# Attention on VectorE: one product instruction for two token columns instead of one for each

## The chip, the cores and the metric

The kernel runs on one core of a Trainium2 chip. The metric is the device time of one execution in microseconds (us); shown are single executions, their median, and one further execution that the hardware profiler recorded. The engines are called as the profile calls them: PE (TensorE, matrix multiplication), DVE (VectorE, elementwise work and reductions), ACT (ScalarE), POOL (GpSimd) and SP (SyncE, which issues most loads).

## The reference

One transformer layer with pre-normalization: 2048 tokens of width 576, 32 heads of 18, everything in fp32. Attention is local and dilated: each token looks at itself and 7 tokens behind it, two positions apart. The MLP is gated by a sigmoid and 4608 wide.

```python
idx = pos[:, None] - off[None, :]            # off = arange(8) * 2
mask = idx >= 0
...
logits = jnp.einsum("bhsd,bhswd->bhsw", q, kg) * scale
logits = jnp.where(mask[None, None, :, :], logits, -1e9)
attn = _softmax(logits, axis=-1)
o = jnp.einsum("bhsw,bhswd->bhsd", attn, vg)
...
h = x + _A_ref(_layernorm(x, axis=-1), A_wqkv, A_wo)
h2 = h + _B_ref(_layernorm(h, axis=-1), B_w_gate, B_w_up, B_w_down)
```

Here `_A_ref` is the attention with its projections, `_B_ref` the MLP.

## The kernel before

With a dilation of two, even and odd tokens never meet, so the sequence is handled as two streams of 1024. Each stream is cut into two halves, which gives four blocks of 512 tokens, numbered 0 to 3 (`BLOCKS`). In a block, each of the 128 partitions holds four tokens that follow one another in the stream (the token columns, `j` = 0 to 3), and K and V of 11 tokens (the four and the seven before them). The heads are handled in four groups of 8 heads, 144 columns each.

`attention` does one block and one group on DVE: for each token column it multiplies a window of 8 K rows by `q` (L174, 128x1152 products), for two columns at a time it sums the products over the head's 18 columns (a reduction, L177), then comes the softmax (L185 to L191, its exponential on ACT at L187), for each column the products of 8 V rows with the weights (L200, again 128x1152), and for two columns at a time three additions (L205, L207, L208). There are 4 blocks x 4 groups = 16 such calls, with 64 K products and 64 V products. The function is a generator: at each `yield` it hands over to the code that interleaves it with other work, so the number of yields in a call sets how attention is spread in the order in which the program is written.

PE's matrix products are made of fp32 numbers split into a high and a low part: `split` lets ACT write the high part (L105) and DVE the low part (L106, source minus high part); `split_rest` does the same for the odd 64 columns (L109, L110). So nearly every matmul needs an earlier ACT and DVE instruction.

In time there are four stages. To about 180 us the kernel makes the layer norm and Q, K, V. From there to about 222 us it makes the output projection and second layer norm of block 0 (the generator `front`; `proj_j` adds the projection to the residual at L245). Then the MLP begins (L576 and L583 are the up and gate products, L694 the down products, L702 their eviction by ACT, L598 to L672 the additions between products). While the MLP of the first tokens runs, attention for the last two blocks is made in its shadow (about 400 to 780 us), and then, in the function `under_rest`, their output projections (`proj_scr`; its operands `th`, `tl` are the split attention output, `wow` a projection weight). After the first projection is written, `under_rest` clears a tile on POOL (L906) and ACT's queue issues two DMAs of these zeros to DRAM (L908).

The program is written in Python order with priorities (`high_priority`), and a list scheduler with a simulated clock decides, when the kernel is built, in which order each engine's instructions stand. On the chip, each engine runs its list in that order; an instruction whose inputs or buffers aren't ready holds up everything behind it on its engine. Most weight buffers have one or two copies: `w2` and `w4` (parts of the MLP's weight slice) have one, `w1` two; `b1`, `b2`, `b3` and `bgp` are PSUM banks of PE.

Of the kernel before, what the change touches and what calls it, by code (L numbers as in the profile page):

```python
# [18 lines left out]
ALU = mybir.AluOpType  # L19
AX = mybir.AxisListType  # L20

P = 128
# [3 lines left out]
DH = 18  # L26
W = 8
# [9 lines left out]
HG = NH // NG  # L37
CG = HG * DH
# [23 lines left out]
def kernel(ctx, tc, x, wqkv, wo, wmlp, out):  # L62
    nc = tc.nc
    dve, act, pool, pe, sp = nc.vector, nc.scalar, nc.gpsimd, nc.tensor, nc.sync
# [92 lines left out]
    def window(s, hf):  # L157
        a = s[hf * TB:hf * TB + TB, :].rearrange("(p j) c -> p (j c)", p=P)
        return bass.AP(tensor=a.tensor, offset=a.offset, ap=[[NS * CG, P], [1, (NS + LP) * CG]])

    def attention(at, b, g, o):
        e, hf = BLOCKS[b]
        q = at.tile([P, NS, CG], F32, name="q")
        kw = at.tile([P, NS + LP, CG], F32, tag="kv", bufs=3, name="kw")
        vw = at.tile([P, NS + LP, CG], F32, tag="kv", bufs=3, name="vw")
        sp.dma_start(q.rearrange("p j c -> p (j c)"), qscr[b][g])
        sp.dma_start(kw.rearrange("p j c -> p (j c)"), window(kscr[e][g], hf))
        sp.dma_start(vw.rearrange("p j c -> p (j c)"), window(vscr[e][g], hf))
        lg = at.tile([P, NS, W, HG], F32, bufs=2, name="lg")
        for u in range(2):  # L170
            pr = at.tile([P, 2, W, CG], F32, name="pr")
            for i in range(2):
                j = 2 * u + i
                dve.tensor_tensor(pr[:, i], kw[:, j:j + W],  # L174
                                  q[:, j].unsqueeze(1).broadcast_to([P, W, CG]), ALU.mult)
                yield
            dve.tensor_reduce(lg[:, 2 * u:2 * u + 2].rearrange("p j w h -> p (j w h)"),  # L177
                              pr.rearrange("p j w (h d) -> p (j w h) d", d=DH),
                              AX.X, ALU.add)
            yield  # L180
        if hf == 0:
            dve.tensor_tensor(lg, lg, mask.unsqueeze(3).broadcast_to([P, NS, W, HG]), ALU.add)
        mx = sm.tile([P, NS, HG], F32, name="mx")
        rs = sm.tile([P, NS, HG], F32, name="rs")
        dve.tensor_reduce(mx, lg.rearrange("p j w h -> p j h w"), AX.X, ALU.max)  # L185
        dve.tensor_tensor(lg, lg, mx.unsqueeze(2).broadcast_to([P, NS, W, HG]), ALU.subtract)
        act.activation(lg, lg, AF.Exp, scale=SCALE)  # L187
        yield
        dve.tensor_reduce(rs, lg.rearrange("p j w h -> p j h w"), AX.X, ALU.add)
        dve.reciprocal(rs, rs)  # L190
        dve.tensor_tensor(lg, lg, rs.unsqueeze(2).broadcast_to([P, NS, W, HG]), ALU.mult)  # L191
        yield
        spill = o is None
        if spill:
            o = kw[:, 0:NS]
        for u in range(2):
            pr = at.tile([P, 2, W, CG], F32, name="pr")
            for i in range(2):
                j = 2 * u + i
                dve.tensor_tensor(  # L200
                    pr[:, i].rearrange("p w (h d) -> p w h d", d=DH),
                    vw[:, j:j + W].rearrange("p w (h d) -> p w h d", d=DH),
                    lg[:, j].unsqueeze(3).broadcast_to([P, W, HG, DH]), ALU.mult)
                yield
            dve.tensor_tensor(pr[:, :, 0:4], pr[:, :, 0:4], pr[:, :, 4:8], ALU.add)  # L205
            yield
            dve.tensor_tensor(pr[:, :, 0:2], pr[:, :, 0:2], pr[:, :, 2:4], ALU.add)  # L207
            dve.tensor_tensor(o[:, 2 * u:2 * u + 2], pr[:, :, 0], pr[:, :, 1], ALU.add)  # L208
            yield
        if spill:  # L210
            pool.dma_start(oscr[b][:, :, g * CG:(g + 1) * CG], o)
            if g == NG - 1:
                pool.dma_start(oscr[b][:, :, D:DX], o[:, :, CG - DR:CG])
# [106 lines left out]
    def load_x(b):  # L320
        e, hf = BLOCKS[b]
        t = sah.tile([P, NS, D], F32, bufs=2, name="h")
        for j in range(NS):
            sp.dma_start(t[:, j], xv[e, hf][:, j])
        return t
# [25 lines left out]
    def qkv_w(g):  # L351
        w = qw_tile("qw")
        if g == 0:
            wr = f32(qw_tile("wr"))[:, 0]
        for c in range(5):
            ws = wr[:, c] if g == 0 else sas.tile([P, NQ], F32, tag="wst", bufs=3, name="ws")
            sp.dma_start(ws, wqkv[g][:, c * NQ:(c + 1) * NQ])
            with tc.high_priority(3 * HI if g == 0 else HI):
                split(w[:, 0, c], w[:, 1, c], ws)
        return w  # L360
# [21 lines left out]
    def att_all():  # L382
        nonlocal o
        for b, g in ((0, 0), (0, 1), (0, 2), (0, 3), (1, 0), (1, 1), (1, 2), (1, 3)):
            while (b, g) not in emitted:
                yield
            if o is None:
                o = tok_tile()
            yield from attention(at, b, g, None if b else o[:, :, g * CG:(g + 1) * CG])
            if (b, g) == (0, 3):  # L390
                for j in range(NS):
                    dve.tensor_copy(o[:, j, D:DX], o[:, j, DM:D])
                ready.append(b)
# [28 lines left out]
    w = [qkv_w(0)]  # L422
# [19 lines left out]
    h = load_x(0)  # L442
# [96 lines left out]
    def d_tile():  # L539
        return gd.tile([P, 2, D], F32R, bufs=4, name="d")  # L540
# [239 lines left out]
    def att_scr(at, blocks):  # L780
        for b in blocks:
            for g in range(NG):
                for _ in attention(at, b, g, None):
                    yield ATT
# [171 lines left out]
    with tc.high_priority(2 * HI):  # L956
        wg2 = load_gu(1, pool)
        d = d_tile()
# [126 lines left out]
    for c, (kind, p, f) in enumerate(items):  # L1085
        w, d = wc
# [40 lines left out]
        else:  # L1127
# [22 lines left out]
            d = M[f]  # L1150
# [55 lines left out]
```

## Time and profile before

| | |
|---|---|
| three runs, median (lowest to highest) | 1584.2 us (1582.86 to 1586.56) |
| the profiled execution's own time | 1582.11 us |
| its span, first to last instruction | 1580.3 us |
| mean granted PE clock | 0.998 |
| PE busy | 1548.5 us, 98% of the span |
| DVE busy | 1257.2 us, 80% |
| ACT busy | 879.8 us, 56% |
| POOL busy | 192.4 us, 12% |

The profile records one execution. "Busy" is the time in which an engine worked on an instruction; the span is what passes between the first and the last of them. The granted clock is the share of its full speed that PE was allowed.

### The profile page before, as it was taken

What the parts mean: (1) busy time and instruction counts of PE and PEld (TensorE: products, weight loads), DVE (VectorE), ACT (ScalarE), POOL (GpSimd) and SP (SyncE); (2) the same over time, 40 slices, a digit from 0 to 9 for tenths busy, and PEclk for the clock granted to TensorE, in tenths of its full rate; (3) what the DMA queues carried; (4) which work ended last, traced back from release to release, by engine and by line L of the source; (5) the groups of instructions that cost most, each with busy time, mean ns of one, the idle gap of its engine ahead of it and who ended that gap; (6) DMA issues with size and microseconds to landing.
All of it is one profiled execution on the core that took longest, in us unless ns stands there. A gap on an engine that the chain in (4) does not pass through costs nothing.

```text
span 1580.3 us, 22467 instructions
## 1 busy us (share of the span) xinstructions
PE 1548.5 (98%) x8532; PEld 1377.6 (87%) x8532; DVE 1257.2 (80%) x1979; ACT 879.8 (56%) x1573; POOL 192.4 (12%) x233
## 2 busy tenths in 40 slices
PE   7999989999999999999999999999999999999998
PEld 6899978898788888888888988888888888888888
DVE  7998999657999999999836678777776777776754
ACT  6422245544555565656543345676766777766772
POOL 2000000000010001000011100111111222121121
PEclk9999999999999999999999999999999999999999
DMA  7555576754476666675785225788798899888987
GB/s 268 192 189 193 191 258 192 199 175 160 129 191 163 159 164 163 179 185 141 203 255 191 97 75 141 149 163 178 154 186 171 172 181 188 176 175 179 175 145 193
DMA packets 77405, 278.23 MB, mean 176 GB/s; under 512 B 7952, under 2 KB 13840, under 8 KB 76400
## 3 DMA queue, kind: packets, MB, share of 16 engines
q0 software_dynamic: 29760, 112.96, 39.0%
q1 hardware_dynamic: 39360, 141.93, 26.4%
q10 hardware_dynamic: 8176, 21.89, 3.7%
q8 instruction: 67, 1.10, 0.3%
q14 instruction: 42, 0.34, 0.1%
HBM read 145.88 MB, written 133.23 MB: 177 GB/s over the span
## 4 chain that ended last, share of the span: by engine, by line
PE 87%; DVE 5%; issue 3%; DMA 2%; ACT 2%; POOL 0%; ACTq 0%; SPq 0%; DVEq 0%; POOLq 0%
PE b L576 42%; PE dp L694 14%; PE dp L766 11%; PE acc L152 8%; PE b L583 8%; PE bgp L152 1%; PE b L152 1%; DMA oj<-o 1%; PE acc L154 1%; PE acc L155 1%; DVE pr L174 1%; DVE w L106 1%; DMA ws<-in_wqkv_dram 1%; DVE lg L177 0%; DVE pr L200 0%
## 5 line engine op out<-in xcount | busy, mean ns | idle before, releaser
L576 PE MATMUL b<-tl,w 128*128 128x512 f32 x1716 | 454.3, 393 | 9.1 <-DVE w L106 5.1
L576 PEld LDWEIGHTS b<-tl,w 128*128 128x128 f32 x1716 | 310.7, 188 | 65.3 <-DVE w L106 5.8
L576 PE MATMUL b<-th,w 128*128 128x512 f32 x1368 | 357.2, 392 | 0.8 <-DVE s L672 0.6
L576 PEld LDWEIGHTS b<-th,w 128*128 128x128 f32 x1368 | 251.3, 188 | 48.7 <-DVE s L672 1.1
L772 ACT ACTIVATE ev<-dp 128x576 f32<-128x576 f32 x224 | 145.8, 651 | 114.8 <-PE dp L766 89.6
L583 PE MATMUL b<-th,w 128*128 128x512 f32 x572 | 179.7, 390 | 0.0
L105 ACT ACTIVATE w<-wg 128x640 fp32r<-128x640 f32 (+2 forms) x197 | 117.0, 596 | 93.2 <-PE b L583 60.0
L106 DVE TENSOR_TENSOR w<-wg,w 128x640 fp32r<-128x640 f32 (+2 forms) x197 | 127.4, 649 | 50.2 <-ACT w L105 49.9
L775 POOL DMA_DIRECT2D h<-ev x128 | 109.1, 852 | 452.0 <-ACT ev L772 441.2
L152 PE MATMUL acc<-qw,th 128*128 128x432 f32 x512 | 154.9, 363 | 1.1 <-ACT qw L105 1.1
L583 PEld LDWEIGHTS b<-th,w 128*128 128x128 f32 x572 | 107.1, 188 | 21.5
L694 PE MATMUL dp<-d,h1h 128*128 128x288 f32 x640 | 123.0, 295 | 0.0
L694 PE MATMUL dp<-d,h0h 128*128 128x288 f32 x640 | 122.5, 295 | 0.3 <-DVE tail L704 0.3
L106 DVE TENSOR_TENSOR w<-tw,w 128x512 fp32r<-128x512 f32 x116 | 79.5, 686 | 38.0 <-ACT w L105 37.9
L694 PEld LDWEIGHTS dp<-d,h0h 128*128 128x128 f32 x640 | 101.5, 188 | 6.3 <-DVE tail L704 0.6
L694 PEld LDWEIGHTS dp<-d,h1h 128*128 128x128 f32 x640 | 101.4, 188 | 5.4
L105 ACT ACTIVATE w<-tw 128x512 fp32r<-128x512 f32 x116 | 73.2, 631 | 53.7 <-PE b L576 41.5
L702 ACT ACTIVATE stage<-dp 128x576 f32<-128x576 f32 x112 | 71.2, 648 | 56.4 <-PE dp L694 55.8
L152 PEld LDWEIGHTS acc<-qw,th 128*128 128x128 f32 x512 | 96.7, 189 | 5.8 <-ACT qw L105 1.4
L369 ACT ACTIVATE ev<-acc 128x432 f32<-128x432 f32 x64 | 33.6, 531 | 112.6 <-PE acc L155 110.4
L152 PE MATMUL acc<-qw,tl 128*128 128x432 f32 x256 | 92.2, 360 | 0.4 <-DVE tl L106 0.4
L672 DVE TENSOR_TENSOR s<-s,b 128x512 f32<-128x512 f32 x58 | 39.6, 683 | 62.3 <-PE b L583 62.2
(278 smaller groups left out, 2955.0 us busy)
## 6 DMA issues: line engine op xcount, KB each, us to landing
h<-ev POOLq DMA_DIRECT2D x96, 576.0 KB, 7.2
wg<-in_wmlp_dram SPq DMA_DIRECT2D x49, 928.0 KB, 6.4
h<-stage POOLq DMA_DIRECT2D x28, 1152.0 KB, 11.4
wg<-in_wmlp_dram SPq DMA_DIRECT2D x36, 640.0 KB, 4.9
kw<-kv SPq DMA_DIRECT2D x16, 792.0 KB, 4.2
vw<-kv SPq DMA_DIRECT2D x16, 792.0 KB, 6.1
wd<-in_wmlp_dram SPq DMA_DIRECT2D x18, 576.0 KB, 8.9
kv<-ev ACTq DMA_DIRECT2D x16, 576.0 KB, 5.8
```

Source lines behind the costliest of these rows:

```text
L105: act.activation(hi, src, AF.Copy)
L106: splits.append(dve.tensor_tensor(lo, src, f32(hi), ALU.subtract))
L152: pe.matmul(ps[:, :n], a[:, c, js], m[:, c], start=k == 0, stop=False)
L369: act.activation(ev[:, :, j], ps[:, :NQ].rearrange("p (t c) -> p t c", t=3), AF.Copy)
L576: pe.matmul(ps, wt[:, a, k0 + c], xx[:, m + c], start=first and k == 0, stop=k == 5, skip_group_check=True)
L583: pe.matmul(ps, wt[:, a, k0], xx[:, 4], start=False, stop=a == 1, skip_group_check=True)
L672: added[0] = dve.tensor_tensor(s2, s2, b3, ALU.add)
L694: pe.matmul(ps[:, i, :DH2], a[:, js], d[:, m, i * DH2:(i + 1) * DH2], start=k == 0, stop=k == n)
L702: act.activation(hv, ps, AF.Copy)
L766: pe.matmul(ps[:, i, :DH2], a[x][:, js], m[y], start=k in (0, 1, 3) and q == 0, stop=q == 2, skip_group_check=True)
L772: act.activation(hs[:, k % 2], ps[:, :, :DH2], AF.Copy)
L775: pool.dma_start(hsev[:, u, k0:k + 1], hs[:, :k + 1 - k0], accum_op=ALU.add, max_dma_last_dim=8 * D)
```

## The change

The two products of a pair of token columns become one instruction, for K and for V. Their windows overlap (column j reads rows j to j+7, column j+1 rows j+1 to j+8), so the new helper `taps` writes an access pattern by hand: a first dimension of two columns, one row (144 elements) apart, over the window of 8 rows. The operands `q` and the weights `lg` are broadcast over two columns at once. Each call of `attention` has 4 product instructions of 128x2304 in place of 8 of 128x1152, and 12 yields in place of 16.

```diff
+    def taps(t, j, n):
+        a = t[:, j:j + W]
+        return bass.AP(tensor=a.tensor, offset=a.offset,
+                       ap=[list(a.ap[0]), [CG, 2], [n, W * CG // n], [1, n]])
+
...
             pr = at.tile([P, 2, W, CG], F32, name="pr")
-            for i in range(2):
-                j = 2 * u + i
-                dve.tensor_tensor(pr[:, i], kw[:, j:j + W],
-                                  q[:, j].unsqueeze(1).broadcast_to([P, W, CG]), ALU.mult)
-                yield
+            dve.tensor_tensor(pr, taps(kw, 2 * u, CG),
+                              q[:, 2 * u:2 * u + 2].unsqueeze(2).broadcast_to([P, 2, W, CG]), ALU.mult)
+            yield
...
             pr = at.tile([P, 2, W, CG], F32, name="pr")
-            for i in range(2):
-                j = 2 * u + i
-                dve.tensor_tensor(
-                    pr[:, i].rearrange("p w (h d) -> p w h d", d=DH),
-                    vw[:, j:j + W].rearrange("p w (h d) -> p w h d", d=DH),
-                    lg[:, j].unsqueeze(3).broadcast_to([P, W, HG, DH]), ALU.mult)
-                yield
+            dve.tensor_tensor(
+                pr.rearrange("p j w (h d) -> p j (w h) d", d=DH), taps(vw, 2 * u, DH),
+                lg[:, 2 * u:2 * u + 2].rearrange("p j w h -> p j (w h)").unsqueeze(3)
+                .broadcast_to([P, 2, W * HG, DH]), ALU.mult)
+            yield
```

With fewer yields and fewer instructions the scheduler writes another order. Line numbers of the changed kernel: K product L177, its reduction L180, maximum L188, subtraction L189, V product L201, additions L206, L208, L209; from there on each line is one further down (L245 becomes L246). The numbers behind a name (`pr_1649`) tell one use of a buffer from another and differ between the two programs.

The first place is DVE ahead of the front, around 170 to 188 us, in the last attention group before it. `wow` is the projection weight that is split there, `tl` the low part of the front's transposed attention output. Before, from the max of the softmax on (the three `wow` splits stand ahead of it) and then from the end of the first V product on:

```order
L106 TENSOR_TENSOR wow_1719<-ws_1728,wow_1719 128x288
L185 TENSOR_REDUCE mx_1584<-lg_1524 128x32
L186 TENSOR_TENSOR lg_1524<-lg_1524,mx_1584 128x256
...
L205 TENSOR_TENSOR pr_1608<-pr_1608 128x2x576
L207 TENSOR_TENSOR pr_1608<-pr_1608 128x2x288
L208 TENSOR_TENSOR kw_1519<-pr_1608 128x288
L106 TENSOR_TENSOR tl_1820<-mm_1821,th_1819 128x4x128
L200 TENSOR_TENSOR pr_1649<-vw_1520,lg_1524 128x1152 x2
L110 TENSOR_TENSOR th_1819<-mm_1861,th_1819 64x128
```

And of the change at the same place:

```order
L188 TENSOR_REDUCE mx_1389<-lg_1347 128x32
L189 TENSOR_TENSOR lg_1347<-lg_1347,mx_1389 128x256
L106 TENSOR_TENSOR wow_1749<-ws_1750,wow_1749 128x288
...
L206 TENSOR_TENSOR pr_1413<-pr_1413 128x2x576
L208 TENSOR_TENSOR pr_1413<-pr_1413 128x2x288
L209 TENSOR_TENSOR kw_1342<-pr_1413 128x288
L201 TENSOR_TENSOR pr_1434<-vw_1343,lg_1347 128x2304
L106 TENSOR_TENSOR tl_1841<-mm_1842,th_1840 128x4x128
L110 TENSOR_TENSOR th_1840<-mm_1882,th_1840 64x128
```

The maximum and the subtraction have moved ahead of the three `wow` splits, and the group's second V product from behind the first `tl` split to ahead of it.

The second place is DVE at the start of the MLP, around 229 to 237 us. `s` is the addition that reads PSUM bank `b2` for the last time before PE writes it again; `w1`, `w4`, `w2` are the low parts of the second weight slice. Before:

```order
L598 TENSOR_TENSOR s_2318<-s_2318,b2_2289 128x512
L177 TENSOR_REDUCE lg_2307<-pr_2308 128x128
L174 TENSOR_TENSOR pr_2322<-kw_2302,q_2301 128x1152 x2
L106 TENSOR_TENSOR w1_2273<-wg_2266,w1_2273 128x640
L106 TENSOR_TENSOR w4_2276<-wg_2266,w4_2276 128x384
L106 TENSOR_TENSOR w2_2277<-wg_2266,w2_2277 128x256
L106 TENSOR_TENSOR w1_2353<-wg_2271,w1_2353 128x640
L177 TENSOR_REDUCE lg_2307<-pr_2322 128x128
```

Of the change:

```order
L180 TENSOR_REDUCE lg_1639<-pr_1640 128x128
L599 TENSOR_TENSOR s_2343<-s_2343,b2_2322 128x512
L177 TENSOR_TENSOR pr_1659<-kw_1634,q_1633 128x2304
L106 TENSOR_TENSOR w1_2306<-wg_2299,w1_2306 128x640
L106 TENSOR_TENSOR w4_2309<-wg_2299,w4_2309 128x384
L180 TENSOR_REDUCE lg_1639<-pr_1659 128x128
L106 TENSOR_TENSOR w2_2310<-wg_2299,w2_2310 128x256
L106 TENSOR_TENSOR w1_2376<-wg_2304,w1_2376 128x640
```

One reduction has moved ahead of `s`, the other ahead of the `w2` split.

The third place is around 812 to 830 us, in `under_rest`, where ACT's queue issues the two DMAs of zeros. ACT before:

```order
L105 ACTIVATE w1_7948<-wg_7601 128x640
L105 ACTIVATE w2_7756<-wg_7486 128x256
L109 ACTIVATE th_7378<-bgp_7702 128x128
L702 ACTIVATE stage_7656<-dp_7833 128x576
L908 DMA h7_100<-stage_8151 128x3x576 x2
L105 ACTIVATE w4_7755<-wg_7486 128x384
```

ACT of the change:

```order
L105 ACTIVATE w1_7884<-wg_7537 128x640
L909 DMA h7_100<-stage_8087 128x3x576 x2
L703 ACTIVATE stage_7592<-dp_7769 128x576
L105 ACTIVATE w2_7692<-wg_7422 128x256
L105 ACTIVATE w4_7691<-wg_7422 128x384
```

The DMA issue has moved ahead of the eviction and of the high part of `w2`. And DVE there, which makes the low parts and the projection's additions to the residual (`hj`, L245); before:

```order
L106 TENSOR_TENSOR w2_7756<-wg_7486,w2_7756 128x256
L110 TENSOR_TENSOR th_7378<-bgp_7702,th_7378 64x128
L245 TENSOR_TENSOR hj_7579<-hj_7579,b3_7706 128x288
L125 BN_STATS bs_7914<-hj_7579 128x6
L245 TENSOR_TENSOR hj_7628<-hj_7628,bgp_7736 128x288
L245 TENSOR_TENSOR hj_7671<-hj_7671,b3_7775 128x288
L598 TENSOR_TENSOR s_7799<-s_7799,b2_7768 128x512
L106 TENSOR_TENSOR w4_7755<-wg_7486,w4_7755 128x384
L106 TENSOR_TENSOR d_7762<-wg_7486,d_7762 128x576
L106 TENSOR_TENSOR h1l_7895<-s_7799,h1h_7894 128x512
L245 TENSOR_TENSOR hj_7700<-hj_7700,bgp_7801 128x288
```

Of the change:

```order
L246 TENSOR_TENSOR hj_7515<-hj_7515,b3_7642 128x288
L125 BN_STATS bs_7850<-hj_7515 128x6
L246 TENSOR_TENSOR hj_7564<-hj_7564,bgp_7672 128x288
L106 TENSOR_TENSOR w2_7692<-wg_7422,w2_7692 128x256
L246 TENSOR_TENSOR hj_7607<-hj_7607,b3_7711 128x288
L246 TENSOR_TENSOR hj_7636<-hj_7636,bgp_7737 128x288
L599 TENSOR_TENSOR s_7735<-s_7735,b2_7704 128x512
L106 TENSOR_TENSOR w4_7691<-wg_7422,w4_7691 128x384
```

The `w2` split, which was ahead of all four residual additions, now has the last two behind it; the addition behind the `w4` split has gone from there.

## Rows read from the trace of the kernel before

**Rows 1.** The page: the span, and each engine's busy time, share and instructions.

```profile
span 1580.3 us, 22467 instructions
...
PE 1548.5 (98%) x8532; PEld 1377.6 (87%) x8532; DVE 1257.2 (80%) x1979; ACT 879.8 (56%) x1573; POOL 192.4 (12%) x233
```

**Rows 2.** Window: PE, PEld, DVE, ACT, POOL busy us; clock, DMA, GB/s.

```profile
440.00:760.00 320.00, 320.00 (x1767) 283.18 (x1767) 303.52 (x410) 186.16 (x309) 27.39 (x26) 1.00 0.65 169
```

**Rows 3.** VectorE's groups by form: shapes, count, busy us, mean ns, idle before.

```profile
L200 DVE TENSOR_TENSOR pr<-vw,lg 128x1152 f32<-128x1152 f32 x64 | 84.2, 1354 | 0.5
L174 DVE TENSOR_TENSOR pr<-kw,q 128x1152 f32<-128x1152 f32 x64 | 84.1, 1352 | 0.4
L177 DVE TENSOR_REDUCE lg<-pr 128x128 f32<-128x2304 f32 x32 | 81.5, 2547 | 0.3
```

**Rows 4.** VectorE's timeline at 102 us: start, us, line, tiles, merged count.

```profile
102.14 2.63 DVE L174 TENSOR_TENSOR pr<-kw,q 128x1152 f32<-128x1152 f32 x2
104.80 2.55 DVE L177 TENSOR_REDUCE lg<-pr 128x128 f32<-128x2304 f32 x1
107.39 2.63 DVE L174 TENSOR_TENSOR pr<-kw,q 128x1152 f32<-128x1152 f32 x2
```

**Rows 5.** VectorE's timeline before and in the front; idle before in brackets.

```profile
169.65 1.20 DVE L106 TENSOR_TENSOR wow<-ws,wow 128x288 fp32r<-128x288 f32 x3 [1.76 <-ACT wow L105]
...
172.37 0.68 DVE L189 TENSOR_REDUCE rs<-lg 128x32 f32<-128x256 f32 x1 [0.49 <-ACT lg L187]
...
174.46 0.46 DVE L106 TENSOR_TENSOR wow<-ws,wow 128x288 fp32r<-128x288 f32 x1 [0.57 <-ACT wow L105]
...
181.40 2.62 DVE L200 TENSOR_TENSOR pr<-vw,lg 128x1152 f32<-128x1152 f32 x2
...
232.74 2.63 DVE L174 TENSOR_TENSOR pr<-kw,q 128x1152 f32<-128x1152 f32 x2
235.29 2.36 DVE L106 TENSOR_TENSOR w<-wg,w 128x640 fp32r<-128x640 f32 x4
```

**Rows 6.** TensorE's timeline in the front and at the MLP's start.

```profile
184.49 0.37 PE L152 MATMUL mm<-wo,th 128*128 128x288 f32 x1 [1.04 <-DVE th L110]
...
222.94 1.52 PE L576 MATMUL b<-tl,th 128*128 128x512 f32 x6
...
226.11 1.52 PE L576 MATMUL b<-tl,th 128*128 128x512 f32 x6
...
236.16 2.08 PE L576 MATMUL b<-tl,w 128*128 128x512 f32 x4 [5.06 <-DVE w L106]
...
240.39 1.07 PE L576 MATMUL b<-tl,w 128*128 128x512 f32 x4
```

**Rows 7.** Windows in the two waits of TensorE; columns as in group 2.

```profile
233.00:239.00 6.00, 2.84 (x7) 2.29 (x8) 6.00 (x7) 1.20 (x2) 0.00 (x0) 0.50 0.92 347
829.00:830.00 1.00, 0.00 (x0) 0.00 (x0) 1.00 (x4) 0.86 (x2) 0.00 (x0) 1.00 1.03 389
```

**Rows 8.** Chain that ended last, 800 to 835 us: start, us, what.

```profile
824.08 2.01 POOL stage L906
...
827.13 0.54 ACT w L105
...
827.69 0.56 DVE w L106
...
829.62 0.38 DVE hj L245
...
830.04 1.85 PE bgp L152 x12
```

**Rows 9.** ScalarE's timeline ahead of the zeroing DMA.

```profile
812.51 0.42 ACT L105 ACTIVATE w<-wg 128x256 fp32r<-128x256 f32 x1 [0.21 <-PE b L576]
...
815.99 0.65 ACT L702 ACTIVATE stage<-dp 128x576 f32<-128x576 f32 x1 [2.63 <-PE dp L694]
```

**Rows 10.** TensorE's timeline at the same place.

```profile
824.01 0.29 PE L152 MATMUL b<-wow,th 128*128 128x288 f32 x1
```

## The prediction

> **What bounds the kernel now.** I read first each engine's busy share, then the windows by stage, then TensorE's waits, and last the timelines around the longest of these. The page shows PE busy for 1548.5 of 1580.3 us [rows 1]: it is the bound, and all its idle time together is 32 us. A change on DVE can gain only what lies in those 32 us; it can lose wherever it makes PE wait more. In the middle of the pair stage, where half of the attention runs, PE is busy for 320.00 of 320 us while DVE has 303.52 [rows 2]: a shorter DVE instruction there only lengthens DVE's idle time. Two places are different. At the MLP's start PE waits 5.06 us, until 236.16 us, for a DVE split [rows 6], behind a DVE that has worked with hardly a gap since 181 us. And near 830 us PE waits for a chain that comes from POOL through ACT's DMA issue to DVE [rows 8]; its end at 830.04 follows the last matmul by 1.86 us.
>
> **The instructions themselves.** 128 products of 128x1152 go, 64 of 128x2304 come. A product takes 1352 to 1354 ns by itself [rows 3], but two in a row take 2.63 us together, and the next instruction starts 2.66 us after the first (102.14 to 104.80) [rows 4]: the second overlaps the first's end and starts 1.28 us after it. A DVE instruction that goes through 2304 elements, the reduction, takes 2547 ns, and the next starts 2.59 us after it (104.80 to 107.39) [rows 3, 4]. For the new product I take this: 0.07 us saved per pair, 64 x 0.07 = 4.5 us of DVE's 1257. Nothing saved at all would be the dear end (a pair at 2.66). A product that is slower because its two windows overlap is bounded by one that takes twice as long per element; I don't expect it, since today's products already read an operand over and over (q eight times, each weight 18 times) and both kinds cost the same 1352 and 1354 ns [rows 3].
>
> [...]
>
> Of the 4.5 us only what stands ahead of a PE wait counts: the seven pairs from 181.40 to 232.74 us (the first and last in [rows 5]), 7 x 0.07 = 0.5 us. The rest lies beside a busy PE.
>
> **The order in the front.** What the new order moves weighs more. Ahead of the front DVE waits 1.76, 0.49 and 0.57 us for ACT [rows 5]. The new order puts the softmax's maximum and subtraction into the first wait and lets the second V product run before the first `tl` split. Filling in the durations, that product ends at about 180.8 us, which is where the split of `tl` (0.6 us, just ahead of 181.40) began before; the 2.6 us from 181.40 on, for which the front's later splits stood behind it [rows 5], are saved, less some 0.2. PE's wait of 1.04 us at 184.49 [rows 6], for the DVE instruction behind that product, goes, and DVE stays about 2.4 us ahead of its old times. Behind the front the same seven pairs, shorter by 0.5, and DVE's lead bring the split for which PE waited until 236.16 to about 236.2 - 2.4 - 0.5 = 233.3. PE's earlier wait, for `s`, grows, because a reduction of 2.55 us now stands ahead of `s`; but it falls into the time in which PE would wait for `w1` anyway. The other reduction now stands ahead of the `w2` split: `w2` is ready at about 236.7, and PE, which does the 12 matmuls between (3.17 us for 14 of them, 222.94 to 226.11, so 2.72 [rows 6]), would get there at 236.1: 0.6 us of new wait, if PE runs at full clock.
>
> The clock is the open part. In the wait of 5.06 us the granted clock fell, and it was 0.50 from 233 to 239 us [rows 7], so that those 12 matmuls took 4.23 us (236.16 to 240.39) [rows 6] instead of 2.72: 1.5 us lost. In the wait near 830 us it stayed at 1.00 [rows 7]. The new wait, some 2.5 us after a shorter one, is between. If the clock falls as before, the gain is 2.8 us (and PE, slow, finds `w2` ready); if it holds, 2.8 + 1.5 - 0.6 = 3.7. I take 3.0. The lower bound is 0.5, the direct part, should the order's lead be lost again to another wait; the upper 3.7.
>
> **The order at 812 to 830 us.** The DMA of zeros waits for POOL's memset, which starts at 824.08 and takes 2.01 us [rows 8], and everything behind it on ACT's queue waits too. Before, the queue held back the high part of `w4`, which came at 827.13; DVE's `w4` split followed at 827.69 and, behind two more splits, the residual addition at 829.62 that freed PE's bank [rows 8]. `w2` had been made at 812.51 and the eviction at 815.99 [rows 9]. Now both are behind the DMA. The chain after it becomes: issue done at about 827.1, eviction 0.65 and `w2` high 0.42 [rows 9], of which the start of the next overlaps some 0.1 each, `w2` low about 0.4 (the 128x384 split of `w4` takes 0.56, an addition 0.38 [rows 8]), and then the two residual additions behind it. The first of these frees bank `b3`, and PE's next block of projection matmuls waits for it: 827.1 + 0.6 + 0.4 + 0.4 + 0.4 = 828.9, say 829.0 us with the signals between. PE comes to that block earlier than the chain: before, it began it at 824.01 [rows 10], and in the new order three L694 matmuls (288 columns against the 512 of [rows 6], so 288/512 x 3.17/14 = 0.13 us each) have moved behind it, so at 823.6. The wait is 5.4 us in place of 1.86: +3.5. Such a wait is as long as the one at 231 us that cost the clock, so I add most of that price, 1.4: **+4.9 us**. The bounds are -1.9 (POOL, which waits for a transfer to land, is free 5 us earlier, and the wait vanishes) and, should the transfer land a microsecond later, +6.
>
> **Elsewhere** the pair stage is scheduled anew. PE is busy in all of 440 to 760 us [rows 2], and behind the third place DVE's and ACT's orders are soon alike again; I put this at 0, plus or minus 1.5, an estimate of the size of the short waits between.
>
> **Sum** on the profiled execution: -3.0 + 4.9 = +1.9, so 1582.1 becomes 1584.0. The profiled execution lay 2.1 us under the median of the runs, so the runs should have a median of 1584.2 + 1.9 = **1586.1 us**. A difference under 0.2% (3.2 us) can't be told from no change: the three runs alone lie 3.7 us apart.
>
> **The rivals.**
> Gain without the new wait: the transfer that POOL waits for lands earlier, or the scheduler's order around it matters less than I think. For it: its landing depends on what else the queues carry, which the order doesn't tell. Against it: the transfers in front of it are the same. Then the front's 3.0 stays: 1581.2; with the old 1.86 gone too, 1579.3.
> Wait without the gain, the slower side: the front finds another wait (the maximum and subtraction ahead of the `wow` splits delay `wow`, or PE waits for `s` behind the reduction), only 0.5 is left, and 4.9 comes: 1588.6. It decides as soon as the front gives back less than 1.7 us.
> Neither, all is hidden: only 0.5 us: 1583.7. That PE is 98% busy speaks for it.
> DVE becomes the bound: the new product is dearer than the pair. Between 440 and 760 us DVE has 16.5 us left [rows 2] for at most the 32 pairs of the last two blocks, so from 0.5 us more per pair on PE waits; at twice the time per element, 2.4 us more per pair, the 64 pairs cost over 100 us: above 1680. Against it: the operands read repeatedly today.
> [...]
>
> **How the numbers follow.** Both terms as worked out: 0.45, own range 1583.5 to 1588.5. Gain alone: 0.22. Wait alone: 0.16. Neither: 0.14. DVE bound: 0.03. The range 1579.3 to 1590 leaves out the last and half a tenth at either end. Faster by over 0.2% (under 1581.0) takes half of the second case and a little of the others: 0.2; slower by over 0.2% (over 1587.4) takes two thirds of the third, a quarter of the first and the last: 0.3; within 0.2%: 0.5.
>
> **What the profile will show.** Products of 2304 elements at 2.5 to 2.6 us each, 64 of them, and DVE's busy time down by about 5 us. PE's wait for the `w` split at the MLP's start ends at about 233.3 and is about half as long. In the chain near 825 us the DMA issue is followed by the eviction, `w2` and a residual addition, and PE's wait there is above 5 us, with a clock under 1.00 behind it. PE's busy time outside these is the same to a few us. I am wrong if the product takes over 2.7 us, if PE's wait at 233 us ends past 235, or if the wait near 825 us is under 3 us.

## The result

The changed kernel takes 1587.74 us in the median (1585.19 to 1590.14, 20 runs), the kernel before 1584.54 us (1581.66 to 1588.94, 20 runs). The ratio is 1.0017, with a 95% interval of 1.0011 to 1.0024: slower by about 2.7 us (the medians are 3.2 us apart). The two profiled executions stand further apart, 1582.11 and 1587.72 us, because the one of before is among its faster ones, 2.4 us under its median, while that of the change lies on its median. The last section comes back to that.

The page of the changed kernel, span and busy times, answers to [rows 1]:

```profile
span 1586.0 us, 22404 instructions
...
PE 1552.4 (98%) x8532; PEld 1380.6 (87%) x8532; DVE 1253.7 (79%) x1915; ACT 878.1 (55%) x1573; POOL 194.3 (12%) x233
```

PE is busy for 3.9 us more, with the same number of matmuls: part of them ran slower, as the windows below show. DVE is busy for 3.5 us less and has 64 instructions less. VectorE's groups by form, as in [rows 3]:

```profile
L201 DVE TENSOR_TENSOR pr<-vw,lg 128x2304 f32<-128x2304 f32 x32 | 81.7, 2555 | 0.6
L177 DVE TENSOR_TENSOR pr<-kw,q 128x2304 f32<-128x2304 f32 x32 | 81.7, 2553 | 0.3
L180 DVE TENSOR_REDUCE lg<-pr 128x128 f32<-128x2304 f32 x32 | 81.5, 2547 | 0.3
```

The new product takes 2.55 us, as long as the reduction over as many elements and 0.07 to 0.08 us less than a pair did [rows 4]. K and V cost the same.

One kind of instruction whose order is the same in both programs shows where the time went: ACT's copy of an MLP product (L624 before, L625 now). There are 31 of them in each kernel. Three in the timeline of ACT before:

```profile
336.00 0.60 ACT L624 ACTIVATE s<-b 128x512 f32<-128x512 f32 x1 [2.53 <-PE b L583]
...
811.08 0.60 ACT L624 ACTIVATE s<-b 128x512 f32<-128x512 f32 x1 [0.27 <-PE b L583]
...
850.61 0.60 ACT L624 ACTIVATE s<-b 128x512 f32<-128x512 f32 x1 [0.18 <-PE b L583]
```

and the same three in the changed kernel:

```profile
334.52 0.60 ACT L625 ACTIVATE s<-b 128x512 f32<-128x512 f32 x1 [2.55 <-PE b L584]
...
811.63 0.60 ACT L625 ACTIVATE s<-b 128x512 f32<-128x512 f32 x1 [0.96 <-PE b L584]
...
855.83 0.60 ACT L625 ACTIVATE s<-b 128x512 f32<-128x512 f32 x1 [0.65 <-PE b L584]
```

At 336 us the change is 1.5 us ahead, at 811 us it is 0.5 us behind, at 851 us 5.2 us. So the front gave 1.5, the stretch from there to 811 us cost 2.0, and the 40 us around 830 cost 4.7.

Around 830 us, the chain of the changed kernel that ended last (as [rows 8]):

```profile
824.19 2.03 POOL stage L907
...
826.65 0.50 ACTq L909
...
827.20 0.04 ACT stage L703
...
827.75 0.42 ACT w L105
...
828.53 0.46 DVE hj L246
...
829.03 3.25 PE b L152 x12
...
832.76 1.79 PE bgp L152 x12
```

and windows of the same stretch (columns as in [rows 2]):

```profile
826.00:827.00 1.00, 0.00 (x0) 0.00 (x0) 0.00 (x0) 0.00 (x0) 0.20 (x1) 0.63 0.00 0
827.00:833.00 6.00, 3.97 (x16) 3.97 (x17) 2.42 (x6) 1.36 (x3) 0.00 (x0) 0.50 0.79 296
```

Behind the memset come the two DMA issues, the eviction, the high part of `w2`, its low part on DVE (828.19, not among the rows shown) and the residual addition, and PE starts its block at 829.03, after a wait of 4.84 us. It was 1.86 before. In the wait the clock falls (0.63 in the window from 826, 0.50 from 827 to 833), and the 12 matmuls of bank `b` in the chain take 3.25 us, where the 12 of the chain of before took 1.85 [rows 8].

At the MLP's start, TensorE's timeline (as [rows 6]):

```profile
183.96 0.40 PE L152 MATMUL mm<-wo,tl 128*128 128x288 f32 x1 [0.44 <-DVE tl L106]
...
221.31 1.54 PE L577 MATMUL b<-tl,th 128*128 128x512 f32 x6
...
230.28 0.70 PE L577 MATMUL b<-tl,w 128*128 128x512 f32 x2 [1.99 <-DVE s L599]
233.39 2.07 PE L577 MATMUL b<-tl,w 128*128 128x512 f32 x4 [2.41 <-DVE w L106]
...
238.67 1.33 PE L577 MATMUL b<-tl,w 128*128 128x512 f32 x4
...
241.70 0.69 PE L695 MATMUL dp<-d,h0h 128*128 128x288 f32 x4
```

DVE's timeline there (as [rows 5]):

```profile
178.19 2.56 DVE L201 TENSOR_TENSOR pr<-vw,lg 128x2304 f32<-128x2304 f32 x1
180.78 0.69 DVE L106 TENSOR_TENSOR tl<-mm,th 128x512 fp32r<-128x512 f32 x1
...
224.39 2.56 DVE L177 TENSOR_TENSOR pr<-kw,q 128x2304 f32<-128x2304 f32 x1
226.98 2.55 DVE L180 TENSOR_REDUCE lg<-pr 128x128 f32<-128x2304 f32 x1
229.45 0.68 DVE L599 TENSOR_TENSOR s<-s,b 128x512 f32<-128x512 f32 x1
...
232.52 1.28 DVE L106 TENSOR_TENSOR w<-wg,w 128x640 fp32r<-128x640 f32 x2
```

and the window that answers to the first of [rows 7]:

```profile
233.00:239.00 6.00, 5.61 (x13) 4.45 (x14) 6.00 (x8) 1.65 (x4) 0.00 (x0) 0.50 0.72 271
239.00:240.00 1.00, 1.00 (x5) 0.76 (x5) 1.00 (x3) 1.00 (x2) 0.00 (x0) 0.91 0.87 186
```

The V product that stood behind the first `tl` split now runs at 178.19, ahead of it; PE's wait of 1.04 us [rows 6] has become one of 0.44 us at 183.96, and the MLP begins at 221.31 instead of 222.94. Its split of `w1` comes at 232.52, and PE resumes at 233.39 instead of 236.16. The wait for `s`, which now stands behind a reduction (229.45 behind 226.98), has grown from 0.49 to 1.99 us, inside the time that PE would have waited for `w1`. But the clock is at 0.50 until 239 us, as before, so the 12 matmuls take 5.28 us (233.39 to 238.67) where they took 4.23 [rows 6].

### The profile page after: what moved, and what is told of

It reads as the page before. It is cut to its first block, busy times and chain, and to the rows that moved or that the text cites. A ratio compares the mean times of both kernels' runs of the same rounds, so it can differ in the third digit from the quotient of the medians.

```text
span 1586.0 us, 22404 instructions
## 1 busy us (share of the span) xinstructions
PE 1552.4 (98%) x8532; PEld 1380.6 (87%) x8532; DVE 1253.7 (79%) x1915; ACT 878.1 (55%) x1573; POOL 194.3 (12%) x233
## 4 chain that ended last, share of the span: by engine, by line
PE 87%; DVE 5%; issue 3%; ACT 2%; DMA 2%; POOL 0%; ACTq 0%; SPq 0%; DVEq 0%; POOLq 0%
PE b L577 41%; PE dp L695 14%; PE dp L767 11%; PE acc L152 8%; PE b L584 8%; PE b L152 1%; PE bgp L152 1%; DMA oj<-o 1%; PE acc L154 1%; PE acc L155 1%; DVE pr L177 1%; DVE w L106 1%; PE b L141 0%; DMA x<-tok 0%; DVE lg L180 0%
```

## The experiments

**The zeros on another queue.** In the changed kernel and in the kernel before, the two DMAs of zeros are issued by POOL, behind its own memset. Both keep the order of every other instruction, so each differs from its parent in this alone.

```diff
             for u in range(2):
-                act.dma_start(hsev[:, u, 1:6:2],
+                pool.dma_start(hsev[:, u, 1:6:2],
```

> The changed kernel with one edit: the two DMAs of zeros are issued from POOL's queue, right behind POOL's own memset, instead of from ACT's. The order of every other instruction is that of the change. Theory A (the new place of the DMA issue on ACT's queue is what makes the change slower): the eviction and the high part of w2 run at about 812 to 816 us, PE's wait of 4.84 us near 829 us and the 4 us at half clock behind it vanish, so 4.84 + 2.0 = 6.8 us less than the change, about 1581, faster than the kernel before. Rival B (the loss sits elsewhere, in the pair stage or in the product): less than 1 us from the change. Rival C (the wait only changes its cause: POOL's queue, now with two more issues, delays the layer norm of the projection): a PE wait of 2 to 4 us stays near 829 us, and the gain is 2 to 4 us.

Measured: 1580.37 us (1578.70 to 1582.76, 11 runs), ratio to the kernel before 0.9976 (0.9967 to 0.9985). That is 7.4 us less than the change by the medians, which were not measured side by side, and 6.5 by the two ratios to the kernel before (1.0017 and 0.9976); 6.8 were expected. Between the marks at 811 and 851 us this run takes 37.3 us (811.45 to 848.73), the change 44.2: 6.9 us less. ScalarE's timeline and, in the second fence, POOL's:

```profile
817.88 0.65 ACT L703 ACTIVATE stage<-dp 128x576 f32<-128x576 f32 x1 [5.20 <-PE dp L695]
818.43 0.41 ACT L105 ACTIVATE w<-wg 128x256 fp32r<-128x256 f32 x1
```

```profile
824.09 2.02 POOL L907 MEMSET stage<- 128x2304 f32 x1 [15.98 <-DMA h<-stage]
826.42 1.52 POOL L909 DMA_DIRECT2D h<-stage  x2 [0.30 <-POOL stage L907]
```

The eviction and `w2` no longer wait for the memset (they ran a few us later than I had written, at 817.88, when their matmuls were done), the memset and the DMAs are where they were, and a window of the same trace shows PE through it without a gap and at full clock:

```profile
822.00:832.00 10.00, 10.00 (x71) 9.65 (x71) 6.78 (x18) 2.84 (x5) 5.78 (x7) 1.00 0.45 159
```

So it is the place on ACT's queue that costs, not the transfer of the zeros or the memset, which are still there. POOL's two additional issues delayed nothing: rival C is out.

> The kernel before with the same edit: the DMAs of zeros on POOL's queue, all other instructions in the order of before. Theory A: PE's wait of 1.86 us at 830 us vanishes, 1.9 us less than the kernel before, about 1582.6. If the kernel before in most executions waits longer there than in the one profiled (its median lies 2.4 us above that execution), up to 4 us less. Rival B or C: within 0.5 us of the kernel before.

Measured: 1582.04 us (1580.69 to 1584.59, 11 runs), ratio 0.9985 (0.9977 to 0.9994), 2.6 us less. The wait of 1.86 us was a real loss in the kernel before too. With the zeros out of the way in both, the change is ahead by 1.7 us (1580.37 against 1582.04, measured side by side; the two intervals overlap a little).

**The pacing and the instruction apart.** First two products per pair, with one yield behind both:

```diff
             for i in range(2):
                 j = 2 * u + i
                 dve.tensor_tensor(pr[:, i], kw[:, j:j + W],
                                   q[:, j].unsqueeze(1).broadcast_to([P, W, CG]), ALU.mult)
-                yield
+            yield
```

(and so for V).

> Two products of 128x1152 for each pair as before, but one yield behind the pair instead of one behind each: the pacing of the change without its instruction. The order that comes out has the front's second V product ahead of the first tl split, as the change has, and ACT's DMA of zeros behind w2, w4 and the high part of h1, with only evictions behind it. Theory A: no PE wait near 830 us (1.86 less than before), the front gains 1 to 1.5 us as in the change, together about 3 us less than before: 1581.5. Rival (the instruction itself makes the difference, not the order): within 1 us of the kernel before, 1584.5.

Measured: 1592.88 us (1590.72 to 1595.03, 5 runs), ratio 1.0052 (1.0040 to 1.0065). The expectation was wrong by 11 us, though the place that it spoke of came out as written: there PE waits 0.2 us (its only wait between 800 and 850 us). Another place appeared. The chain around 340 us:

```profile
321.79 16.97 DMA wg<-in_wmlp_dram
...
338.77 0.74 ACT w L105
...
341.80 0.31 DVE th L110
...
342.15 0.47 PE b L145
```

On SP's queue a weight slice of the MLP (`wg`) was issued at 321.79, behind nine loads for the projection of block 1, and landed 17 us later; ACT's split of it held up DVE, and PE waited 3.4 us for a `th` rest that stood behind that split. Two more waits for ACT, 4.0 us together, follow between 380 and 410 us. Behind both places PE ran at about half its pace: six L576 matmuls from 344.56 us took 2.76 us, where six took 1.52 at full clock [rows 6], and 16 from 404.77 took 6.15. The mean clock was 0.66 from 340 to 350 and from 400 to 410 us, and 1.00 in the 10 us ahead of each and behind. So this order has a loss of its own, and the run does not tell the pacing from the instruction; the next one does.

Then the new product with 16 yields:

```diff
             dve.tensor_tensor(pr, taps(kw, 2 * u, CG),
                               q[:, 2 * u:2 * u + 2].unsqueeze(2).broadcast_to([P, 2, W, CG]), ALU.mult)
             yield
+            yield
```

(and so for V).

> One product of 128x2304 for each pair as in the change, but two yields behind it, so 16 in each call as before: the instruction of the change with the pacing of before. In the order that comes out, ACT's DMA of zeros stands ahead of w2 as in the change, and so do the front's pieces. Theory A: PE waits 4.8 us near 829 us at half clock afterwards, and the time is that of the change, 1587.5, within 1 us. Rival (the fewer yields are the cause): the time of the kernel before, 1584.5.

Measured: 1588.11 us (1586.04 to 1589.50, 11 runs), ratio 1.0023 (1.0014 to 1.0032): the change's time. TensorE's waits between 800 and 850 us:

```profile
PE b L152 <- DVE hj L248: 5.0, 1, 5.0
```

So the wait doesn't come from the fewer yields: both orders that have the DMA ahead of `w2` have it, with 12 yields and with 16.

**Half of the change.** Only K, or only V, gets the new product. Both halves come out with the DMA of zeros behind `w2`, as before.

> Half of the change: one 128x2304 product per pair for K, two of 128x1152 for V as before; 14 yields per call. In the order that comes out, ACT's DMA of zeros stands behind w2 and the eviction, as in the kernel before, and the w2 split of the MLP's second slice stands ahead of the reduction. Theory A: PE's wait near 829 us is back to about 1.9 us with no loss of clock, the front gains 1 to 2 us: 1582 to 1583.5. Rival (the product of 2304 elements itself, through its overlapping reads, slows something): half of the change's loss, 1586.

Measured: 1581.30 us (1579.56 to 1583.73, 12 runs), ratio 0.9977 (0.9967 to 0.9987).

> The other half: one 128x2304 product per pair for V, two for K as before; 14 yields. ACT's DMA of zeros stands behind w2 and the eviction, as before. Theory A: as with K alone, a wait of about 1.9 us near 829 us, 1582 to 1583.5. Rival (the product itself): 1586.

Measured: 1581.12 us (1578.46 to 1583.63, 11 runs), ratio 0.9976 (0.9967 to 0.9985). Each half is faster than the kernel before by 3.5 to 3.7 us, a little more than expected; both together are slower. That rules out the product itself, since each half contains it. A wait near 827 us is there in both, 1.82 and 1.35 us, as expected; but in the K half the clock fell behind it, which was not expected (the last section has the window).

**The MLP's start.** The change with the zeros on POOL, and the first K product of one attention call held behind DVE's `w2` split. `tie` is set when the second slice's weights are written, and the call yields until then. Beside the edit that moves the zeros:

```diff
+            if (b, g, u) == (1, 2, 0):
+                while not tie:
+                    yield
+            with tc.issue_after(tie[0]) if (b, g, u) == (1, 2, 0) else ExitStack():
+                dve.tensor_tensor(pr, taps(kw, 2 * u, CG),
...
             wc = weights(items[c + 1][0], raws.pop(0), c + 1 < NF + NSTD)
+            tie.append(splits[-2].ins)
```

> The change with the zeros on POOL's queue, and one more edit: the first K product of the attention call (block 1, group 2) may only be issued behind DVE's w2 split for the MLP's second weight slice. On DVE, s, w1, w4 and w2 then stand directly behind the front's last attention additions, ahead of two products and two reductions. Theory A2 (at the MLP's start the change still loses to PE's two waits, and to the half clock that they bring on and that stays until about 239 us whenever they end): both waits, 1.99 and 2.41 us in the change, vanish with the 2.8 us lost to the clock; at the front up to 7 us less than the run with only the zeros moved, of which the later attention may give back some 2 us near 300 to 420 us: 1574 to 1576. Rival (the clock falls at the MLP's start for another reason, whatever PE waits): the waits go, the clock window of 0.50 stays, 4 us less: 1576.5. Rival (DVE's attention is late, and its projection makes PE wait again between 300 and 440 us): no gain.

Measured: 1579.37 us (1578.45 to 1580.23, 5 runs), ratio 0.9968 (0.9956 to 0.9980): 1.0 us under the run with the zeros moved alone, not 4 to 7, and the two intervals overlap, so no gain shows. Windows and, in the second fence, TensorE's timeline:

```profile
233.00:239.00 6.00, 5.35 (x25) 4.20 (x24) 5.45 (x6) 3.27 (x7) 0.00 (x0) 1.00 0.97 372
380.00:390.00 10.00, 4.01 (x17) 2.72 (x17) 9.77 (x12) 5.80 (x7) 1.23 (x1) 0.82 0.83 191
```

```profile
386.00 0.55 PE L582 MATMUL b<-tl,w 128*128 128x512 f32 x1 [4.41 <-ACT tl L106]
387.74 0.79 PE L582 MATMUL b<-tl,w 128*128 128x512 f32 x1 [1.19 <-ACT tl L106]
```

The first part of the theory held: without the waits the clock stays at 1.00 from 233 to 239 us. The rest is the last rival of the expectation: DVE's attention is late, and nearly all of the gain goes again. The sums that ACT splits into the next MLP operands (`tl`) came later, the first of them (`rs`, L272) at 383.64 us where it came at 380.42 with the zeros moved alone; PE waited 4.41 and 1.19 us for the splits, and there the clock fell instead (0.82 in the window from 380).

**Half the change without the wait.** The V half with the zeros on POOL; all else in the V half's order.

> The V half of the change, and the DMAs of zeros on POOL's queue; the order of all other instructions is that of the V half alone. Theory A: PE's wait of 1.35 us near 826 us and, in the executions in which the clock falls behind it, up to 2 us more go: 1.4 to 2.5 us less than the V half alone, about 1579. That would put half of the change with the zeros moved level with the whole change with the zeros moved (1580.4) or under it, so that the other half's instruction buys nothing that can be measured. Rival (the 2304-element product is worth time on DVE by itself, 64 times 0.07 us): the whole change with the zeros moved is the faster one by 2 us.

Measured: 1577.70 us (1577.17 to 1579.27, 5 runs), ratio 0.9964 (0.9950 to 0.9977), the lowest ratio of all. It stands 0.0012 under that of the V half alone, 1.9 us, inside the 1.4 to 2.5 that were expected, though the two intervals overlap (the medians, 3.4 us apart, come from different chips). It also stands 0.0012 under that of the whole change with the zeros moved; those intervals overlap too, so the other half's instruction buys nothing that shows.

## Why the prediction was right, and where its sizes were off

The forecast was +1.9 us, 1586.1 in the median; measured were 1587.7, and 1.0017 as a ratio, +2.7 us. The mechanism at the third place was right, but that the sum came so near was in part luck. On the two profiled executions, for which the sum was made, the terms measured below add up to -1.5 + 2.0 + 4.7 = +5.2 us, and the executions differ by 5.6, where +1.9 was forecast: the gain in the front was put at twice what it gave, and the losses elsewhere at nothing. The medians differ by less because the profiled execution of before is a fast one.

**The instruction.** Taken at 2.59 us from start to start, a pair at 2.66. In the trace after, 2.55 us alone and 2.59 us from start to start (the product at 224.39 and the reduction at 226.98). DVE's two kinds of product went from 168.3 to 163.4 us, 4.9 us less, against 4.5 forecast. Two products in a row overlap (2.63 us for a pair [rows 4], where one alone takes 1.35), so the sum of their lengths is not what the pair costs: twice 1.35 exceeds the 2.55 of the new product by 0.15 us, a pair by 0.08.

**The front.** The step "The order in the front" is the term that was mis-sized: 3.0 us forecast, 1.5 measured. Its order part was right almost to the tenth: the product ends at about 180.8 us, PE's wait of 1.04 us shrinks to 0.44, and PE resumes at 233.39 where 233.3 was written. What failed is the sentence on the clock, that a clock that falls as before costs what it cost before. It was at 0.50 from 233 to 239 us in both [rows 7], so PE, which resumed 2.8 us earlier, did in those 2.8 us at half speed what takes 1.4: of the 2.8 us half is left, and 1.5 us is the lead at 336 us. The 2.8 us for the case that the clock falls assumed that the stretch at half clock moves along with PE's return; it did not. PE's wait began at about the same time in both (at 231.1 and 231.0 us, by the rows), and the half clock ended at about 239 us in both (0.94 before and 0.91 in the change in the window from 239 to 240). The run with the front held shows the other side: no wait of PE above 0.6 us between 225 and 245 us, and the clock at 1.00.

**The third place.** Forecast: `w2` behind the DMA, a wait of 5.4 us in place of 1.86, and a falling clock, together +4.9. Measured: 4.84 us, PE resuming at 829.03 where 829.0 was written (it came to the wait 0.6 us later than written), and half clock for the 3.97 us that PE worked between 827 and 833, 2.0 us lost: 3.0 + 2.0 = +5.0 from the rows, +4.7 by the marks at 811 and 851 us. That this place makes the change slower is shown by moving the DMA away (6.9 us less between the two marks, and then faster than the kernel before), and from the other side by the two halves, which leave it where it was.

**Elsewhere.** Put at 0, plus or minus 1.5; it was +2.0 between 336 and 811 us, outside these bounds. Some 0.9 of it is idle time in new short waits: between 440 and 811 us PE waits five times, 1.3 us together, where it waited once, 0.4 us. The part up to 760 us shows in the window that was full before [rows 2]:

```profile
440.00:760.00 320.00, 319.36 (x1758) 281.91 (x1757) 300.16 (x383) 183.07 (x305) 27.37 (x26) 1.00 0.65 169
```

The other 1.1 is what these waits cost beyond their idle time. The rows of the changed kernel around one of them:

```profile
525.87 0.29 PE L695 MATMUL dp<-d,h0h 128*128 128x288 f32 x1
526.49 1.65 PE L577 MATMUL b<-tl,w 128*128 128x512 f32 x6 [0.32 <-DVE s L599]
```

Matmuls in a row overlap: four of the first kind take 0.69 us (the row at 241.70 above), and one by itself 0.29, so in a row they start 0.13 us apart. Here one starts 0.62 us ahead of the next matmul, 0.17 more than 0.13 and the idle 0.32; and the six behind the wait take 1.65 us where six take 1.54 without one (the row at 221.31). That is 0.28 us on top of the idle time. The experiments agree. Between the marks at 811 and 851 us the kernel before takes 39.53 us and without its wait of 1.86 us 37.40, 2.13 less; the V half takes 39.02 and without its wait of 1.35 us 37.40, 1.62 less. Four waits more at 0.27 us each make the 1.1.

**The rivals.** The gain without the new wait did not come by itself, but it is what the DMA on POOL's queue makes (0.9976). The wait without the gain was half true: the front gave 1.5 of its 3.0, less than the 1.7 that the prediction named as the mark for this rival, whose 1588.6 lies nearer to the measured median than the forecast does. DVE as the bound and a dearer product are ruled out by the 2.55 us and by the two halves; the twofold time per element in that rival was the author's assumption, which no run shows.

## What to carry to other kernels

Where a scheduler orders the instructions, a change that spares DVE some 0.08 us per pair of products, as this one does, also deals the order anew, and the order can be worth more than the instruction: six orders of nearly the same work took from 1581.1 to 1592.9 us here. Look in the new order for an instruction on a busy queue that waits for a slow engine or a transfer (here a DMA issue on ACT that waits for POOL's memset) and at what has come to stand behind it; put such a wait on a queue whose next work doesn't matter, before judging the change. And a wait of PE cost more than its length here: some 0.27 us because the matmuls around it don't overlap (four waits between 440 and 811 us, and those of 1.35 and 1.86 us near 830), and where the clock fell in it, 2.0 us near 830 us and, at the MLP's start of the change, half of the 5.61 us that PE worked at 0.50, 2.8 us.

## What the runs showed of the hardware

In these runs the clock did not answer to a wait's length alone. The kernel before and the kernel before with the zeros on POOL have the same order up to 800 us, and at the same place, near 405 us, both have a wait of nearly the same length. TensorE's timeline of before, and in the second fence that of the run with the zeros moved:

```profile
405.53 3.01 PE L576 MATMUL b<-tl,w 128*128 128x512 f32 x12 [1.77 <-DVE s L598]
408.38 0.62 PE L583 MATMUL b<-th,w 128*128 128x512 f32 x2
```

```profile
407.02 4.24 PE L576 MATMUL b<-tl,w 128*128 128x512 f32 x12 [1.79 <-DVE s L598]
411.05 1.04 PE L583 MATMUL b<-th,w 128*128 128x512 f32 x2
```

The 12 matmuls behind it took 2.85 us in one (405.53 to 408.38) and 4.03 us in the other (407.02 to 411.05), where the clock fell (0.63 in the window from 408 to 410 us, 0.52 from 410 to 412; 1.00 from 406 to 410 in the trace of before). This loss did not reach the end, though. To the same matmul further on it is 16.82 us in both, from 405.53 to 422.35 and from 407.02 to 423.84:

```profile
422.35 1.66 PE L576 MATMUL b<-tl,w 128*128 128x512 f32 x6 [0.17 <-ACT s L658]
```

```profile
423.84 1.65 PE L576 MATMUL b<-tl,w 128*128 128x512 f32 x6
```

At full clock PE ran into three more short waits for DVE and ACT there (0.64, 0.15 and 0.17 us), at half clock it did not. The K half alone shows a fall near 829 us: a wait of 1.82 us and then a window at 0.50,

```profile
829.00:830.00 1.00, 1.00 (x6) 1.00 (x5) 0.54 (x2) 0.00 (x0) 0.79 (x1) 0.50 1.05 334
```

where the kernel before kept 1.00 in a wait of 1.86 us [rows 7]. Here it did cost: between the marks at 811 and 851 us the K half takes 41.02 us, 1.5 more than the kernel before with a wait as long. So waits of about 1.8 us sometimes cost the clock here and sometimes not. In the MLP it fell behind each wait of 2.8 us and more: to 0.50 in the kernel before (5.06 us), near 830 us in the change and in the run with one product and 16 yields (4.84 and 5.0), in the run with the front held (4.41), and in the two runs of the V half (2.9 and 2.8, each soon followed by another of 2.0 and 2.1); in the run with two products PE's pace halved behind 3.39 us. The wait of 2.41 us in the change stands 0.70 us behind one of 1.99, and behind this pair the clock was at 0.50 too, from 233 to 239 us. Shorter ones were enough in two traces: near 68 us all ten have a wait of about 1.3 us (1.32 before) and soon one of about 0.4, and behind them the clock fell in two (0.57 from 70 to 74 us in the run with one product and 16 yields, a mean of 0.91 from 60 to 80 in the run with two products) and stayed at 1.00 in eight. It fits that single runs of one kernel lie up to 7 us apart (1581.66 to 1588.94 for the one before), and that the profiled execution of before, in which both of its waits of 1.8 us kept the clock, is 2.4 us under the median of its runs. That the spread comes from there was not measured by itself; the one such fall whose cost can be read, in the K half, took 1.5 us.
